# First loads on two queues, w4 in the place of an earlier weight, six output buffers, and a new operation order in an attention and MLP block

## The chip, the cores and the metric

The kernel runs on one core of a Trainium2 chip. The metric is the device time of one execution in microseconds (us); lower is better.

## The reference

One sequence of 2048 rows with 448 features in bf16 goes through two residual blocks. The first is attention over a short sliding window (16 heads of 28 features, 8 keys at distances 0, 2, ... 14 back); the second normalises, mixes neighbouring rows by shifting four groups of features, and ends in an MLP.

```python
S, D, F, H, W, dil = 2048, 448, 1792, 16, 8, 2
# block A
q, k, v = split_heads(layernorm(x) @ wqkv)            # wqkv: 448 x 1344
idx = s - 2*j, j = 0..7, masked where negative
logits[s, j] = (q[s] . k[idx]) * Dh**-0.5
h = x + concat_heads(softmax(logits) @ v[idx]) @ wo   # wo: 448 x 448
# block B
g = gelu(layernorm(h) @ w1)                            # w1: 448 x 448
# the four quarters of g's columns are shifted by +1, -1, +2, -2 rows
x1 = h + shifted(g) @ w2                               # w2: 448 x 448
y = x1 + gelu(layernorm(x1) @ w3) @ w4                 # w3: 448 x 1792, w4: 1792 x 448
out = h + y
```

All eight inputs and the output are bf16 in HBM.

## The kernel before

**Operations and their order.** The kernel is first written down as 891 operations, each one instruction or a short group of instructions on one engine, and only then put in order. `_Sched.add` and `group` record an operation with its dependences; `ORDER` (line 19 on) is one long list of operation numbers, and each engine (PE, the vector engine DVE, ACT, POOL, and SP, which issues the DMAs) executes its own operations in that order, waiting on semaphores for the others. Because every instruction is emitted in one helper, nearly all have the line L994 in the profile; they are told apart by the names of their tiles. `OTHER` (line 51 on) lists operations that are given to a second choice of engine: a copy out of PSUM goes from ACT to DVE (`copy`), the product that ends a softmax from DVE to POOL, one normalisation of four from ACT to DVE. Numbers in `ORDER` and `OTHER` count the operations as they are recorded; w4's two loads are recorded at another place after the change, so that the same operation can have another number there.

**Stages.** The rows are handled in four parts t of 512 rows (four tiles of 128). For each part the operations are recorded in these phases, whose names the text uses with the part's number behind them:

- N1: the first layer norm. DVE's bn_stats and bn_aggr per tile (`ln_stats`), a power on ACT or POOL, the normalisation into `lntm`. In part 0 the work is done tile by tile: tile 0, tile 1, and tiles 2 and 3 together (`FIRST`).
- A1: transposition of `lntm` on PE into `actT`, with copies out of PSUM (`transposed`, `transposed_single`), and the matmuls for q and k with `wqkv_s`, evicted into the arena. V is the same for v, evicted to `vt`; `vw<-vt` are four DMA transfers per part (named vwp, vwa, vwb, vwc) that lay v out by window.
- A2: four products of q with shifted k on DVE (`qk_r`) and their sums over features on PE. S: the softmax on these logits; its last product writes `pb` from the exponentials and the inverse sums, and PE turns it.
- A3: four block-diagonal products on DVE (`bd_r`), PE's matmuls of these with `vw`, copies to `actT`. O: the matmul with `wo_s` and the first residual, added by PE in parts 0 and 1 and by DVE in parts 2 and 3, into `xin`.
- B1: the second layer norm, whose `lntm` is transposed by a DMA (`dma_start_transpose` on SP) into `actT`. M: the matmuls with w1 and gelu, into the arena.

After these come five units u of 2, 4, 4, 4 and 2 tiles:

- B2: the matmul with w2 and the second residual into `xb` in the arena; T: the third layer norm and its transposition by DMA.
- W3: 14 groups of matmuls with w3, each followed by a gelu on ACT into `h3T`.
- B3: the matmul with w4, and DVE's scalar_tensor_tensor into an output buffer `ost`, which SP's DMA stores. There are `NO` = 3 such buffers.

The names T0 or B11 stand for the phase and its part or unit: B11 is phase B1 of part 1, T0 is phase T of unit 0. The order written in `ORDER` interleaves the phases of different parts, so that one part's DVE work stands beside another part's matmuls.

**Buffers.** Tiles come from pools of fixed size (eight PSUM banks, two `lntm`, four `actT`, two `qk_r`, three `bd_r`, sixteen `h3T`, three `ost`); `arrange` hands them out in the order of `ORDER`, and an operation that takes a used buffer waits for the operations that last used it. The weights w3, wqkv with a rearranged copy of part of it (`wr_s`), and w4 lie side by side in one arena in SBUF (`A_W3`, `A_W`, `A_W4`).

**DMAs.** All DMAs are issued by SP, in `ORDER`'s order: x in six pieces (x0 and x1 of one tile, x2, x4 and x6 of two, x8 and x12 of four), the q and k columns of wqkv in two halves (wqka, wqkb), the v columns in two (wv), then wo, w1, w2, w3 in two halves of 896 KB and w4 in two of 784 KB. `load_x` and `load_rows` (lines 428 to 436) record them. `arrange` ties the transposing DMAs to the others on SP:

```python
if op.insts[0][0] == "dma_start_transpose":
    op.deps.update(turned + moved)
    turned, moved = [op], []
elif op.is_dma and not callable(op.chan):
    op.deps.update(turned)
    moved.append(op)
```

A transposing DMA waits until every load and every `vw` transfer that stands ahead of it since the last transposition has landed, and those that stand behind it wait for it. Stores of the output are left out of this. In the order before, the first DMAs are x0, x1, x2, wqka, wqkb, x4, x6 and the two of wv; w3 and w4 stand after the loads of part 0, w4's ahead of T0's transposition.

**Tables.** ACT loads a function table when it goes from exponentials and logarithms to gelu or back; `emit_engine` asks for the first of the two (line 989), the other load is put in by the compiler (line 994).

Of the kernel before, what the change touches and what calls it, by code (L numbers as in the profile page):

```python
# [5 lines left out]
ACT = mybir.ActivationFunctionType  # L6
# [9 lines left out]
NBD, NLN, NACT, NSM, NO = 3, 2, 4, 1, 3  # L16
# [33 lines left out]
"""  # L50
OTHER = """
104 127 196 197 199 402 408 411 519 525 528 582 583
# [229 lines left out]
def bass_sequential_preLN__sliding_local_dilated__mixer_s_mlp__prompt_kernel(  # L282
# [20 lines left out]
    MOVED = {0: (64, 48, 3), 1: (96, 32, 4), 2: (64, 16, 3)}  # L303


    A_W3 = 0
    A_W = A_W3 + 4 * 1792
    A_W4 = A_W + 4 * (1344 + 128)
    A_QG = A_W4 + NF * 448
    QGW = SEQ + 4  # L310
    A_KV = A_QG + 4 * QGW
    KVB = 4 * D * 2
    A_END = A_KV + NST * KVB
    assert 4 * KVW + 1024 <= KVB

    with ExitStack() as es:
# [111 lines left out]
        def load_x(i, n):  # L428
            return dma("x%d" % i, xin[:, i:i + n, :], xv[:, i:i + n, :], 128 * n * D * 2)
# [606 lines left out]
```

## Time and profile before

| | us |
|---|---|
| median of 3 runs | 193.6 |
| lowest and highest run | 193.39, 193.7 |
| span of the profiled execution | 192.0 |
| busy in that span, PE | 181.2 |
| busy, ACT | 133.0 |
| busy, DVE | 129.6 |
| busy, POOL | 29.3 |
| busy, PE's weight loads (beside its matmuls) | 92.6 |

The span runs from the first to the last instruction that the hardware profiler recorded; for the profiled execution this span is its only time, and the runs above are timed without a profile. PE is TensorE, DVE is VectorE, ACT is ScalarE, POOL is GpSimd and SP is SyncE, whose queue (SPq) issues DMAs. In the profile's lines `out<-in` are the program's names of the tiles, `128x512` is partitions by elements, `x4` is the number of instructions, and `<-` names what ended a wait. The granted clock is a share of TensorE's full speed. Inferred waits name what came last.

### The profile page before, as it was taken

How to read it: one execution, taken by the hardware profiler on the slowest of the kernel's cores; microseconds unless marked ns; L12 is line 12 of the kernel's file. 1: busy time of each engine (PE TensorE's matmuls, PEld its weight loads, DVE VectorE, ACT ScalarE, POOL GpSimd, SP SyncE). 2: the span in 40 equal slices, each digit the busy share in tenths (PEclk: the TensorE clock that was granted, in tenths of full speed). 3: DMA queues.
4: the chain of work that ended last, by engine and by line, in shares of the span. 5: the costliest groups of instructions: out<-in, count | busy, mean ns of one | idle time of the engine just before them, and what ended most of it. 6: DMA issues, size and time to landing. Idle time of an engine off the chain costs nothing.

```text
span 192.0 us, 5741 instructions
## 1 busy us (share of the span) xinstructions
PE 181.2 (94%) x2482; PEld 92.6 (48%) x2482; DVE 129.6 (67%) x229; ACT 133.0 (69%) x310; POOL 29.3 (15%) x63
## 2 busy tenths in 40 slices
PE   6999999999999869969999999999999999999994
PEld 2584533453444333337545444455444544555672
DVE  7899999999999999999876970036988022002203
ACT  4489999999999999998595898860158004731340
POOL 3240000000004000201067000022077700000000
DMA  5998792005504163935905014006200542000111
GB/s 146 353 282 175 194 295 44 14 0 133 133 3 90 23 66 72 319 64 125 113 3 106 8 34 103 0 0 126 58 26 1 109 106 73 0 3 0 51 48 48
DMA packets 30273, 17.04 MB, mean 89 GB/s; under 512 B 18936, under 2 KB 29736, under 8 KB 30248
## 3 DMA queue, kind: packets, MB, share of 16 engines
q1 hardware_dynamic: 30248, 16.68, 37.1%
q8 instruction: 19, 0.31, 0.7%
q14 instruction: 6, 0.05, 0.1%
HBM read 8.04 MB, written 1.84 MB: 51 GB/s over the span
## 4 chain that ended last, share of the span: by engine, by line
PE 67%; DMA 13%; ACT 12%; DVE 3%; SPq 2%; issue 1%; POOL 0%; POOLq 0%; ACTq 0%
PE ps L994 67%; DMA actT<-lntm 7%; DMA arena<-in_B_w_dram 3%; ACT lntm L994 3%; ACT arena L994 3%; DMA vw<-vt 2%; ACT vt L994 2%; SPq L994 2%; DVE bd_r L994 2%; ACT h3T L994 1%; ACT actT L994 1%; ACT xin L994 1%; DVE lntm L994 1%; DVE ost L994 1%; ACT ls L994 1%
## 5 line engine op out<-in xcount | busy, mean ns | idle before, releaser
L994 PE MATMUL ps<-actT,arena 64*128 64x256 bf16 (+1 forms) x756 | 68.7, 329 | 2.2 <-DMA actT<-lntm 1.7
L994 ACT ACTIVATE h3T<-ps 128x512 bf16<-128x512 f32 (+1 forms) x70 | 30.3, 525 | 40.1 <-PE ps L994 40.0
L994 PEld LDWEIGHTS ps<-actT,arena 64*128 64x128 bf16 x756 | 35.4, 94 | 31.6 <-DMA actT<-lntm 2.1
L994 PE MATMUL ps<-arena,h3T 64*128 64x448 bf16 (+2 forms) x434 | 44.4, 343 | 0.0
L994 ACT ACTIVATE arena<-ps 128x512 bf16<-128x512 f32 (+10 forms) x86 | 40.1, 515 | 3.3 <-PE ps L994 2.5
L994 DVE SCALAR_TENSOR_TENSOR ost<-ps,mrs,arena 128x448 bf16<-128x448 f32 (+1 forms) x17 | 10.7, 652 | 36.5 <-PE ps L994 36.5
L994 DVE TENSOR_TENSOR qk_r<-arena 128x4096 bf16<-128x4096 bf16 (+1 forms) x16 | 32.0, 2016 | 0.4 <-ACT arena L994 0.2
L994 PEld LDWEIGHTS ps<-arena,h3T 64*128 64x128 bf16 (+1 forms) x434 | 23.0, 94 | 18.7 <-issue 0.2
L994 POOL TENSOR_TENSOR arena<-arena,xin 128x448 f32<-128x448 f32 x16 | 17.2, 1088 | 45.0 <-DVE lntm L994 45.0
L994 DVE TENSOR_TENSOR bd_r<-arena,bmask 80x2048 bf16<-80x2048 bf16 x16 | 19.0, 1216 | 1.6 <-PE ps L994 0.9
L994 ACT ACTIVATE actT<-ps 128x512 bf16<-128x512 f32 (+2 forms) x21 | 14.6, 742 | 2.1 <-PE ps L994 2.1
L994 PE MATMUL ps<-actT,w_s 64*128 64x512 bf16 x112 | 13.3, 377 | 1.7 <-DMA actT<-lntm 1.2
L994 PE MATMUL ps<-wo_s,actT 64*128 64x448 bf16 x128 | 14.3, 350 | 0.1
L994 PE MATMUL ps<-arena,actT 64*128 64x448 bf16 x112 | 12.4, 350 | 0.4 <-ACT vt L994 0.4
L994 PE MATMUL ps<-w_s,arena 64*128 64x448 bf16 x112 | 11.6, 350 | 1.0 <-ACT arena L994 0.9
L994 ACT ACTIVATE lntm<-xin,nm 128x448 bf16<-128x448 bf16 x16 | 10.5, 660 | 2.6 <-DVE nm L994 2.6
L994 DVE SCALAR_TENSOR_TENSOR arena<-xin,rs_y,ps 128x448 f32<-128x448 bf16 x16 | 10.3, 672 | 2.2 <-PE ps L994 2.2
L994 DVE TENSOR_SCALAR lntm<-arena,mv,rs_y 128x512 bf16<-128x512 f32 x14 | 10.2, 773 | 2.1 <-POOL rs_y L994 2.0
L994 POOL TENSOR_TENSOR pb<-ls,mx 128x512 bf16<-128x512 f32 x2 | 3.3, 1641 | 52.8 <-ACT mx L994 52.8
L994 DVE BATCH_NORM_STATS2 st<-xin 128x6 f32<-128x448 bf16 x16 | 9.4, 614 | 0.8 <-DMA xin<-in_A_x_dram 0.7
L994 PEld LDWEIGHTS ps<-actT,w_s 64*128 64x128 bf16 x112 | 5.1, 94 | 8.9 <-PE ps L994 1.7
L994 PEld LDWEIGHTS ps<-wo_s,actT 64*128 64x128 bf16 x128 | 5.6, 94 | 6.7 <-PE ps L994 1.4
(73 smaller groups left out, 161.7 us busy)
## 6 DMA issues: line engine op xcount, KB each, us to landing
arena<-in_B_w_dram SPq DMA_DIRECT2D x2, 896.0 KB, 7.3
out_dram<-ost SPq DMA_DIRECT2D x15, 112.0 KB, 1.9
arena<-in_B_w_dram SPq DMA_DIRECT2D x2, 784.0 KB, 5.7
vw<-vt SPq DMA_DIRECT2D x4, 320.0 KB, 4.3
vw<-vt SPq DMA_DIRECT2D x4, 256.0 KB, 4.2
arena<-in_A_wqkv_dram SPq DMA_DIRECT2D x2, 448.0 KB, 4.6
xin<-in_A_x_dram SPq DMA_DIRECT2D x2, 448.0 KB, 7.5
xin<-in_A_x_dram SPq DMA_DIRECT2D x3, 224.0 KB, 5.6
```

The source lines that it names most:

```text
L994: inst = getattr(eng, meth)(**kw)
```

## The change

The first two loads of x and the two halves of the q and k weights alternate between SP's and ACT's DMA queues: x0 and wqka on SP, x1 and wqkb on ACT; x2 follows wqka on SP, where before it came ahead of it. The first exponential on ACT, which loads a table, and DVE's bn_stats are ordered behind the second half's issue (`odeps`: order only, without a wait; DVE's bn_stats only have to stand behind it in `ORDER`). All loads are ordered one behind the other whatever their queue.

w4 is placed where wqkv and `wr_s` lie (`A_W4 = A_W`), and its two loads are recorded after phase V of part 3, the last that reads those weights; they wait for that. There are six output buffers in place of three.

`ORDER` is a new list throughout, and `OTHER` too. By `OTHER`, eight copies out of PSUM go from ACT to DVE (one of the two for `actT` of tiles 2 and 3 in A10, four in the evictions of q and k, two in A32, one of V3) and four from DVE to ACT (the other of A10's two, one in A32, two in A33). The last products of S0 and S1 go from DVE to POOL, so that all four are there. In B10 one normalisation goes to DVE and another to ACT. ACT has ten table loads where it had twelve. Some steps change places with their neighbours: a bn_stats of tile 4 stands ahead of the normalisations of tiles 2 and 3; B11's normalisations stand behind one block-diagonal product more; T0's normalisations stand ahead of A23's last product of q and k, and six groups of W30's matmuls ahead of PE's sums of that product. SP's order becomes x0, wqka, x2, x4, x6, wv, x8, x12, `vw` of parts 0 and 1, wo, w1, w2, w3's first half, B10's transposition, w3's second half, B11's, T0's, w4's first half, part 3's four `vw` transfers, w4's second half, B12's transposition, T1's, and the rest.

The diff, without the middle of the two order lists:

```diff
--- before.py
+++ after.py
@@ -13,43 +13,43 @@
 TURN = {'A1': 'tttt', 'B1': 'dddd', 'B2': 'ddddd'}
 NORM = {'N0': 'vvvv', 'N1': 'avvv', 'B1': 'avvv', 'B2': 'avvvv'}
 STATS = {'N1': 'vvva', 'B1': 'avaa', 'B2': 'avvvv'}
-NBD, NLN, NACT, NSM, NO = 3, 2, 4, 1, 3
+NBD, NLN, NACT, NSM, NO = 3, 2, 4, 1, 6
 POWER = {'N1': 'aaaa', 'B1': 'aaaa', 'B2': 'apapp'}
 RESIDUAL = 'ttvv'
 ORDER = """
-43 8 7 2 11 0 1 49 44 45 6 9 10 12 5 39 13 40 42 58 59 60 61 63 64 62 70 68 50 51 52 53 54 55 56 57 14 65 66 71 69 67
...
+37 5 0 1 6 7 4 2 38 47 48 49 50 51 52 53 54 55 8 9 10 11 56 57 61 58 59 62 39 60 63 64 40 95 96 97 65 98 100 99 105 13
...
 """
 OTHER = """
-104 127 196 197 199 402 408 411 519 525 528 582 583
+104 125 127 159 195 196 197 251 278 354 363 400 406 412 415 493 519 582 583
 """
 FULL = (4,)
 FILL = (1, 1, 0, 0)
@@ -305,8 +305,8 @@
 
     A_W3 = 0
     A_W = A_W3 + 4 * 1792
-    A_W4 = A_W + 4 * (1344 + 128)
-    A_QG = A_W4 + NF * 448
+    A_W4 = A_W
+    A_QG = A_W4 + max(NF * 448, 4 * (1344 + 128))
     QGW = SEQ + 4
     A_KV = A_QG + 4 * QGW
     KVB = 4 * D * 2
@@ -425,20 +425,21 @@
         xv = x2.rearrange("(i p) d -> p i d", p=128)
         ov = o2.rearrange("(i p) d -> p i d", p=128)
 
-        def load_x(i, n):
-            return dma("x%d" % i, xin[:, i:i + n, :], xv[:, i:i + n, :], 128 * n * D * 2)
-
-        def load_rows(chan, dst, src, lo, n):
+        def load_x(i, n, eng="sp"):
+            return dma("x%d" % i, xin[:, i:i + n, :], xv[:, i:i + n, :], 128 * n * D * 2, eng)
+
+        def load_rows(chan, dst, src, lo, n, engs=("sp", "sp")):
 
             for h in range(2):
-                dma("%s%s" % (chan, "ab"[h]), dst[:, 2 * h:2 * h + 2, :], src[192 * h:192 * h + 256, lo:lo + n].rearrange("(c k) n -> k c n", k=128), 256 * n * 2)
+                dma("%s%s" % (chan, "ab"[h]), dst[:, 2 * h:2 * h + 2, :], src[192 * h:192 * h + 256, lo:lo + n].rearrange("(c k) n -> k c n", k=128), 256 * n * 2, engs[h])
 
         S.tag = "load"
-        for i in range(2):
-            load_x(i, 1)
+        for i, eng in enumerate(("sp", "act")):
+            load_x(i, 1, eng)
+        load_rows("wqk", wqkv_s[:, :, 0:2 * D], A_wqkv, 0, 2 * D, ("sp", "act"))
+        begun = S.ops[-1]
         load_x(2, 2)
-        act(zs[:, 0, 0:1], epsilon[:, 0:1], ACT.Exp)
-        load_rows("wqk", wqkv_s[:, :, 0:2 * D], A_wqkv, 0, 2 * D)
+        act(zs[:, 0, 0:1], epsilon[:, 0:1], ACT.Exp).odeps.add(begun)
         load_x(4, 2)
         load_x(6, 2)
         load_rows("wv", wqkv_s[:, :, 2 * D:3 * D], A_wqkv, 2 * D, D)
@@ -453,13 +454,9 @@
         for k, (lo, c, src, n) in enumerate(((0, 2, 368, 80), (80, 2, 0, 48), (0, 3, 48, 64), (64, 3, 48, 64))):
             dma("w2%d" % k, w2_s[lo:lo + n, c, :], B_w2[src:src + n, :], n * D * 2)
         load_rows("w3", w3_s, B_w3, 0, F)
-        w4_v = B_w4.rearrange("(f k) n -> k f n", k=128)
-        for f in range(0, NF, 7):
-            dma("w4%d" % f, w4_s[:, f:f + 7, :], w4_v[:, f:f + 7, :], 128 * 7 * D * 2)
-        for eng in ("sp", "pool", "act"):
-            loads = [op for op in S.ops if op.tag == "load" and op.eng == eng]
-            for a, b in zip(loads, loads[1:]):
-                b.odeps.add(a)
+        loads = [op for op in S.ops if op.is_dma]
+        for a, b in zip(loads, loads[1:]):
+            b.odeps.add(a)
 
         TOP, BOT = slice(0, 64), slice(64, 128)
 
@@ -495,7 +492,7 @@
 
         def ln_stats(kind, src_ap, i):
             st = _Tile(P_st)
-            dve("bn_stats", out=st(), in_=src_ap)
+            dve("bn_stats", out=st(), in_=src_ap).odeps.add(begun)
             dve("bn_aggr", out=mv[:, kind, i, :], in_=st())
 
         def sums_stats(kind, tiles, src, ln, at=0):
@@ -870,6 +867,11 @@
         UNITS = [range(0, 2), range(2, 6), range(6, 10), range(10, 14), range(14, 16)]
         b2_a = {}
 
+        def load_w4():
+            w4_v = B_w4.rearrange("(f k) n -> k f n", k=128)
+            for f in range(0, NF, 7):
+                dma("w4%d" % f, w4_s[:, f:f + 7, :], w4_v[:, f:f + 7, :], 128 * 7 * D * 2)
+
         def phase_B2(u):
             tiles = UNITS[u]
             summed = STATS["B2"][u] == "a"
@@ -965,6 +967,9 @@
                 for name, phase in phases:
                     S.tag = "%s%d" % (name, t)
                     phase(t)
+                    if S.tag == "V%d" % (NST - 1):
+                        S.tag = "w4"
+                        load_w4()
                     if S.tag == "N10":
                         last = S.ops[-1]
                         S.tag = "late"
```

58 rows, old and new, of the table ORDER are left out of this document.

## The prediction

> **What bounds the kernel now.** I read the page first, then the busy time by window, then the chain of waits, then the timeline at the few places where the chain leaves the matmuls.
>
> ```profile
> span 192.0 us, 5741 instructions
> PE 181.2 (94%) x2482; PEld 92.6 (48%) x2482; DVE 129.6 (67%) x229; ACT 133.0 (69%) x310; POOL 29.3 (15%) x63
> ...
> 0.00:8.19 8.19, 6.23 (x27) 2.74 (x28) 6.29 (x18) 4.41 (x11) 1.67 (x12) 1.00 0.76 228
> 0.00:8.81 8.81, 6.85 (x39) 3.36 (x41) 6.52 (x19) 4.50 (x11) 2.25 (x14) 1.00 0.78 238
> 0.00:58.98 58.98, 56.25 (x921) 27.94 (x922) 55.93 (x85) 52.72 (x139) 5.25 (x37) 1.00 0.55 144
> 0.00:74.18 74.18, 68.47 (x1165) 33.56 (x1165) 70.89 (x109) 67.58 (x171) 7.46 (x38) 1.00 0.54 129
> 0.00:85.71 85.71, 77.98 (x1256) 37.01 (x1257) 81.73 (x130) 78.94 (x197) 8.78 (x40) 1.00 0.55 135
> 0.00:96.07 96.07, 87.85 (x1494) 44.06 (x1494) 90.73 (x145) 86.44 (x218) 10.02 (x42) 1.00 0.56 132
> 15.00:57.00 42.00, 41.30 (x739) 18.58 (x733) 41.69 (x46) 41.73 (x112) 0.00 (x0) 1.00 0.45 110
> 96.00:189.00 93.00, 92.93 (x986) 48.30 (x987) 37.99 (x84) 46.66 (x93) 19.26 (x21) 1.00 0.20 45
> ```
>
> A window's row has start and end, length, the busy time (and instructions) of PE, PE's weight loads, DVE, ACT and POOL, then the granted clock, the DMA engines' share and GB/s. A row from zero gives an engine's work done by then, and time less work is its idle time so far. For PE that is 1.96 us at 8.19, 2.73 at 58.98, 5.71 at 74.18, 7.73 at 85.71 and 8.22 at 96.07. Then it stops: 92.93 of the next 93 us are busy. So the kernel's time is PE's work (181.2), PE's idle time up to 96 us (8.2), and a tail after the last matmul (192.0 - 181.2 - 8.2 = 2.6, the last store). The change alters no matmul and keeps the last stores in their order, so work and tail stay; **only the 8.2 can move**. From 15 to 57 us PE, DVE and ACT are busy 41.30, 41.69 and 41.73 of 42.00: nothing there can swallow a delay. The chain shows where the rest of the 8.2 arises:
>
> ```profile
> 67.50 1.29 DVE lntm L994 x4
> ...
> 68.82 5.27 DMA actT<-lntm
> ...
> 76.09 6.49 DMA arena<-in_B_w_dram
> ...
> 82.60 3.06 DMA actT<-lntm
> ...
> 90.60 5.43 DMA actT<-lntm
> ...
> 96.07 92.72 PE ps L994 x981
> ```
>
> DVE's work (B11's normalisations, to 68.79) sets when B11's transposing DMA starts (68.82); w4's second half, ahead of T0's on SP, sets when that one starts (82.60); B12's starts at 90.60 and PE runs freely from 96.07.
>
> The three runs shown have a median of 193.6; the profiled execution has its span alone, 192.0, so 1.6 us are taken as lying around the span.
>
> **The first loads.** They gain no bandwidth: x0 to x6 and wqk are one stretch of a full DMA system.
>
> ```profile
> 2.00:8.81 6.81, 6.57 (x39) 3.23 (x39) 5.60 (x18) 3.30 (x11) 1.15 (x5) 1.00 0.99 305
> ...
> 0.81 1.34 SPq L994 DMA_DIRECT2D xin<-in_A_x_dram  x3
> ...
> 3.95 0.29 ACT L994 ACTIVATE rs_x<-mv,epsilon 128x1 f32<-128x1 f32 x1 [1.65 <-DVE mv L994]
> ...
> 6.80 0.70 DVE L994 TENSOR_SCALAR lntm<-xin,mv,rs_y 128x448 bf16<-128x448 bf16 x2 [0.32 <-ACT rs_y L994]
> ...
> 7.99 0.42 DVE L994 COPY actT<-ps 128x512 bf16<-128x512 bf16 x1 [0.17 <-PE ps L994]
> 8.19 5.81 PE L994 MATMUL ps<-actT,arena 64*128 64x256 bf16 x98 [0.24 <-issue]
> 8.81 2.34 DVE L994 BATCH_NORM_STATS2 st<-xin 128x6 f32<-128x448 bf16 x4 [0.39 <-DMA xin<-in_A_x_dram]
> ```
>
> The DMA engines are busy 0.99 of the time, so what is issued earlier only lands ahead of something else. The Trainium skill, DMA: Bandwidth & Descriptors, section Issuing engines are not separate DMA queues, says the same of any pair of queues: the transfers interleave on the same 16 engines and only issue time is saved. By that rule x4 lands no earlier than now; by the opposite it would land about 1 us sooner, and the sum below would be 1.1 lower. No run here shows two queues.
>
> x4 lands at about 8.8 now (DVE waits for it until 8.81), and x0, x1, wqk, x2, x4 are the same bytes in the new order, so 8.8 stays. But x2 now follows half of wqk on SP's queue, and the new order puts a bn_stats of tile 4 ahead of the normalisations of tiles 2 and 3. DVE then waits for x4 with two normalisations (0.70) and a copy (0.42) undone: 6.52 - 0.70 - 0.42 = 5.40 of work at 8.85, idle 3.45 instead of 2.29, **1.1 us worse**. PE does 24 matmuls on tiles 0 and 1 (24 x 5.81/98 = 1.4; work 6.23 + 1.4 = 7.65), then waits for the actT copies of tiles 2 and 3: stats 9.4, normalised 10.1, turned and copied 11.3; idle 3.65 instead of 1.96. Bounds: 0 if x2 and x4 land a microsecond earlier, 2 if x2 falls behind all of wqk and x4 behind both. I take 1.1, by x4's row.
>
> ```profile
> L989 ACT ACT_TABLE_LOAD x6 | 7.7, 1283 | 0.9 <-PEq L1021 0.8
> ```
>
> ACT's own two issues cost 2 x 0.45 us (1.34/3 on SP) ahead of its table load (1.28): 0.8 + 0.9 + 1.3 = 3.0, before its first use of the variance at 3.95. Free; at three times the price it would be 0.9 late.
>
> **The order on DVE up to 80 us.** Adding the durations along the new list, DVE has these amounts ahead of each milestone:
>
> ```profile
> L994 DVE CAST actT<-ps 128x512 bf16<-128x512 f32 x4 | 2.7, 683 | 0.0
> L994 DVE TENSOR_TENSOR pb<-ls,mx 128x512 bf16<-128x512 f32 x2 | 1.4, 682 | 0.0
> L994 DVE TENSOR_TENSOR bd_r<-arena,bmask 80x2048 bf16<-80x2048 bf16 x16 | 19.0, 1216 | 1.6 <-PE ps L994 0.9 <-ACT arena L994 0.6
> L994 POOL TENSOR_TENSOR pb<-ls,mx 128x512 bf16<-128x512 f32 x2 | 3.3, 1641 | 52.8 <-ACT mx L994 52.8
> ...
> 57.27 1.05 DVE L994 TENSOR_SCALAR lntm<-xin,nm,rs_y 128x512 bf16<-128x512 bf16 x3
> ...
> 63.60 3.67 PE L994 MATMUL ps<-actT,w_s 64*128 64x512 bf16 x28 [0.77 <-DMA actT<-lntm]
> ...
> actT<-lntm SPq DMA_TRANSPOSE x9, 4.4
> ```
>
> To B10's last normalisation: five more PSUM copies net (0.1 to 0.68 each, 2.1 together), two softmax products given to POOL (-1.2 net of overlap): +0.9. To B11's last: a block-diagonal product (1.14 net) comes ahead as well: +2.1. To A23's last product: +3.9, as another copy (0.6), T0's normalisations (0.9) and two of O2's sums (1.2) come ahead too; PE's work ahead of its use grows by 2.5 (W30's first six groups). To T0's normalisations: -2.9.
>
> The products on POOL take 1.64 on the mean against 0.68. S0's stands between ACT's last exponential and PE's turn with no cover left, and the three engines feed one another from 15 to 57 us without slack, so a delay of one becomes a delay of all. Between 0 and 0.6 us is carried on; I take 0.5. DVE's idle time, 3.05 at 58.98 now, becomes 3.05 + 1.1 + 0.5 = 4.65.
>
> ```profile
> 78.21 1.23 DVE L994 TENSOR_TENSOR qk_r<-arena 128x2048 bf16<-128x2048 bf16 x1
> 79.35 1.00 DVE L994 TENSOR_SCALAR lntm<-arena,nm,rs_y 128x512 bf16<-128x512 f32 x2
> ...
> 80.36 0.40 PE L994 MATMUL ps<-qk_r,zc 128*32 128x512 bf16 x4
> ```
>
> Then, by DVE's present end, its added work and the 1.6 of idle time, with PE's work ahead in brackets:
> B10 is normalised at 58.3 + 0.9 + 1.6 = 60.8 (the row at 57.27 ends at 58.32) and transposed in 4.4; M0 at 65.3, where now it is 63.60. PE's idle time there is 2.73 + 0.77 = 3.5 now, its work 60.1; half a microsecond of that goes behind M0: 65.3 - 59.6 = 5.7.
> B11 at 68.8 + 2.1 + 1.6 = 72.5; 5.27 more, M1 at 77.8 (68.5 + 1.7 of O2 moved ahead = 70.2): idle 7.6, now 5.71.
> T0 at 80.35 - 2.9 + 1.6 = 79.0 and, w4 no longer being ahead of it, transposed in 3.06; W30 at 82.1 (it stands 3.9 of work earlier, 78.0 - 3.9 = 74.1): idle 8.0, now 7.73.
> A23's product at 79.4 + 3.9 + 1.6 = 84.9 (80.36 - 5.7 + 2.5 = 77.1): idle 7.8.
>
> **w4, w1 to w3.** w4's 1.6 MB leave T0's way: the stall at 85.71 is no longer theirs. But the loads of w1, w2 and w3a now stand on SP just ahead of B10's transposition, w3b between it and B11's, and w4 with V3's four vw transfers between T0's and B12's. A transposition waits for every load issued before it.
>
> ```profile
> arena<-in_B_w_dram SPq DMA_DIRECT2D x2, 896.0 KB, 7.3
> arena<-in_B_w_dram SPq DMA_DIRECT2D x2, 784.0 KB, 5.7
> ```
>
> w3b is issued at 65.3 and lands 7.3 later, 72.6, just when B11 is normalised: 0. w4a goes at 82, w4b behind the vw issues at 86; it lands 5.7 to 7 later, 92 to 93. B12: PE ends its B21 group at 79.7 of work, 87.7; DVE has 5.6 from there to B12's last normalisation, 93.3, and 5.43 later, at 98.8, PE has done 90.7: idle 8.1. A33's products, 5 us of DVE work behind, need 8.1 as well. The four vw transfers could put w4b's landing 0 to 2 later; I take 0, since DVE ends as late.
>
> **The rest.**
>
> ```profile
> L994 DVE SCALAR_TENSOR_TENSOR ost<-ps,mrs,arena 128x448 bf16<-128x448 f32 (+1 forms) x17 | 10.7, 652 | 36.5 <-PE ps L994 36.5
> ```
>
> Six output buffers: DVE's wait ahead of ost, 36.5, is all for PE, none for a store, so more of them give 0. Two of the twelve table loads (1.28 each) go, both after 96 us where ACT is busy 46.66 of 93: 0.
>
> **The sum.** Five waits now end at 7.6 (M1), 7.8 (A23), 8.0 (T0), 8.1 (B12) and 8.1 (A33) of idle time. Each is good to half a microsecond; the time goes by the latest, which of five near-equal ones lies about 0.6 above their level of 7.9. With 0.2 for short waits where the new order brings other instructions together (the 8.22 at 96.07 now stands half a microsecond over the 7.73 of T0's wait, by such) that is 8.7 against 8.2: span 192.5, **194.1 us**, slower by 0.26%; alone it ends between 193.3 and 194.9. A difference under 0.2% (0.4 us) can't be told from none here.
>
> **Rivals.** (1) The start costs nothing: x2 and x4 land a microsecond sooner, since wqk is issued at 1.3 instead of 2.2 and 2.7. Then all five waits fall by 1.1: idle 7.6, 193.0 us (192.3 to 193.2), as T0's wait for w4 is gone and nothing has replaced it. Against it: the 0.99. (2) Slower, by one mechanism: w4b and the four vw transfers land after B12 is normalised. It decides from 93.3 us on; each microsecond later is one on the time, as PE's order has nothing else left, 195.3 at 94.5 (194.8 to 196). For it: 2.2 MB go in that stretch, against 6.49 us for w4b alone in the chain. Against it: at the 305 GB/s of the first stretch they need 7.2 us. (3) The gaps close: PE's idle time between 57 and 96 us, 5.5 now, shrinks to 0.5, on the 2.73 + 1.7 brought along: 4.9, 190.3 us. Against it: DVE's four microseconds more ahead of A23's product. (4) The change doesn't bring its loads earlier at all: that is the forecast's own start, as it counts on no bandwidth.
>
> The Trainium skill, SBUF — State Buffer, section Who interferes with whom, has an exclusive lock between GpSimd and a DVE product of two SBUF operands, the later one waiting. The trace agrees: the POOL product that started inside a q·k product took 2.2 us, the one beside bn_stats 1.1.
>
> ```profile
> 58.98 2.28 DVE L994 TENSOR_TENSOR qk_r<-arena 128x4096 bf16<-128x4096 bf16 x1
> ...
> 59.99 2.21 POOL L994 TENSOR_TENSOR pb<-ls,mx 128x512 bf16<-128x512 f32 x1 [47.99 <-ACT mx L994]
> ...
> 86.13 1.07 POOL L994 TENSOR_TENSOR pb<-ls,mx 128x512 bf16<-128x512 f32 x1 [4.84 <-ACT mx L994]
> ```
>
> By that rule S1's product, which stands beside q·k products, takes the 2.2; with 1.1 the carried 0.5 would be 0 and the time 193.6.
>
> **How the numbers follow.** Forecast 0.45 (0.32 slower, 0.13 the same), the free start 0.29 (0.28 faster, 0.01 the same), late w4 0.19 (slower), the closed gaps 0.07 (faster). That makes faster 0.35, the same 0.14, slower 0.51. From 192.3 to 196.0 these are held but for their edges and the last, which is left out.
>
> **What would show it.** Right: DVE's bn_stats of tile 4 near 8.8 with the normalisations of tiles 2 and 3 behind it; a PE gap of about 2 us near 9; PE idle 3.6 by 12 us; M0 near 65, M1 near 77.8, W30 near 82; PE without gaps from about 99; no wait of DVE for a store. Wrong: tiles 2 and 3 normalised before 9, PE's idle time at 57 us below 3.2, or a single wait after 85 us of over 1 us.

## The result, and the profile after

The kernel after the change takes 196.75 us (median of 4 executions, 196.30 to 197.48) against 193.65 before: ratio 1.0149, 95% interval 1.0114 to 1.0184. It is slower by 1.5%. The forecast was 194.1 with a range from 192.3 to 196.0. Executions of a kernel that took over 1.5% longer than its fastest are left out of the ratios, and of the counts further down.

The page of the profiled execution (196.55 us) first, then its busy time by window. The windows are those shown of before; the columns are time, length, busy us (instructions) of PE, PE's weight loads, DVE, ACT and POOL, the granted clock, the DMA share and GB/s.

```profile
span 194.5 us, 5754 instructions
PE 181.8 (93%) x2482; PEld 93.1 (48%) x2482; DVE 128.2 (66%) x231; ACT 130.9 (67%) x304; POOL 33.7 (17%) x65
```

```profile
0.00:8.81 8.81, 6.31 (x35) 2.50 (x35) 6.08 (x17) 4.05 (x10) 1.08 (x10) 1.00 0.83 270
0.00:58.98 58.98, 53.78 (x853) 27.45 (x853) 53.70 (x81) 48.70 (x128) 10.39 (x39) 1.00 0.48 129
0.00:74.18 74.18, 65.59 (x1136) 32.92 (x1138) 67.91 (x105) 62.72 (x159) 11.47 (x40) 1.00 0.46 122
0.00:85.71 85.71, 75.99 (x1248) 37.87 (x1250) 79.33 (x128) 73.69 (x183) 12.70 (x42) 1.00 0.45 116
0.00:96.07 96.07, 86.07 (x1390) 43.67 (x1392) 87.98 (x144) 83.73 (x209) 15.03 (x46) 1.00 0.49 127
96.00:189.00 93.00, 92.83 (x1075) 47.46 (x1071) 38.70 (x85) 47.27 (x96) 18.72 (x19) 1.00 0.24 50
```

Time less PE's work is PE's idle time: 2.50 us at 8.81 (1.96 before), 5.20 at 58.98 (2.73), 8.59 at 74.18 (5.71), 9.72 at 85.71 (7.73) and 10.00 at 96.07 (8.22). So PE is 2.5 us behind by 59 us, stays 1.8 to 2.9 behind, and from 96 us on it is busy without a gap in both kernels. Most of the loss is not where the prediction looked, among the waits from 60 to 96 us, but in one place ahead of them. The windows from 45 to 55 us show it, before first:

```profile
45.00:55.00 10.00, 9.93 (x180) 4.41 (x178) 9.90 (x10) 9.90 (x31) 0.00 (x0) 1.00 0.52 121
```

```profile
45.00:55.00 10.00, 8.08 (x98) 3.66 (x98) 7.76 (x7) 7.59 (x25) 4.03 (x1) 1.00 0.76 177
```

PE, DVE and ACT each lose 2 us, and POOL works 4. The timeline of the kernel after (start, length, engine; in brackets the idle time before and what ended it), DVE, POOL and PE from 44 us:

```profile
44.25 2.29 DVE L999 TENSOR_TENSOR qk_r<-arena 128x4096 bf16<-128x4096 bf16 x1
46.45 0.62 DVE L999 CAST vt<-ps 128x448 bf16<-128x448 f32 x1
46.98 2.29 DVE L999 TENSOR_TENSOR qk_r<-arena 128x4096 bf16<-128x4096 bf16 x1
51.50 1.22 DVE L999 TENSOR_TENSOR bd_r<-arena,bmask 80x2048 bf16<-80x2048 bf16 x1 [2.23 <-ACT arena L999]
...
46.18 4.03 POOL L999 TENSOR_TENSOR pb<-ls,mx 128x512 bf16<-128x512 f32 x1 [9.53 <-ACT mx L999]
...
50.35 0.49 PE L999 MATMUL ps<-ident,pb 64*80 64x64 bf16 x16 [1.86 <-POOL pb L999]
```

S1's last product, which the change gave to POOL, starts at 46.18 while DVE multiplies q by k, and ends at 50.21, 0.94 after DVE's second such product (49.27). PE waits 1.86 us to turn its result, ACT copies that, and DVE waits 2.23 us for the copy. All three lose the same two microseconds in a row.

### The profile page after: what moved, and what is told of

It is laid out like the page before. It is cut to its first block, busy times and chain, and to the rows that moved or that the text cites. A ratio compares the mean times of both kernels' runs of the same rounds, so it can differ in the third digit from the quotient of the medians.

```text
span 194.5 us, 5754 instructions
## 1 busy us (share of the span) xinstructions
PE 181.8 (93%) x2482; PEld 93.1 (48%) x2482; DVE 128.2 (66%) x231; ACT 130.9 (67%) x304; POOL 33.7 (17%) x65
## 3 DMA queue, kind: packets, MB, share of 16 engines
HBM read 8.04 MB, written 1.84 MB: 51 GB/s over the span
## 4 chain that ended last, share of the span: by engine, by line
PE 57%; DVE 28%; ACT 6%; DMA 4%; POOL 2%; issue 1%; SPq 0%; ACTq 0%
PE ps L999 57%; DVE qk_r L999 9%; DVE lntm L999 4%; DVE bd_r L999 4%; DVE st L999 3%; DVE arena L999 3%; DMA xin<-in_A_x_dram 3%; ACT actT L999 2%; POOL pb L999 2%; ACT arena L999 2%; DMA actT<-lntm 2%; DVE mx L999 1%; DVE actT L999 1%; DVE mv L999 1%; DVE ost L999 1%
## 5 line engine op out<-in xcount | busy, mean ns | idle before, releaser
L999 PE MATMUL ps<-actT,arena 64*128 64x512 bf16 (+1 forms) x756 | 70.4, 329 | 1.7 <-DMA actT<-lntm 0.8
L999 PE MATMUL ps<-arena,h3T 64*128 64x448 bf16 (+2 forms) x434 | 45.1, 343 | 0.1
L999 ACT ACTIVATE arena<-ps 128x512 bf16<-128x512 f32 (+10 forms) x83 | 39.2, 505 | 5.1 <-PE ps L999 4.2
L999 ACT ACTIVATE actT<-ps 128x512 bf16<-128x512 f32 (+2 forms) x22 | 15.2, 715 | 6.3 <-PE ps L999 6.1
L999 POOL TENSOR_TENSOR pb<-ls,mx 128x512 bf16<-128x512 f32 x4 | 7.3, 1815 | 56.2 <-ACT mx L999 34.6
L999 PE MATMUL ps<-actT,w_s 64*128 64x512 bf16 x112 | 14.0, 377 | 0.3
L999 DVE TENSOR_SCALAR lntm<-arena,mv,rs_y 128x512 bf16<-128x512 f32 x14 | 7.5, 593 | 3.0 <-ACT rs_y L999 1.9
L999 PE MATMUL ps<-bd_r,vw 80*32 80x64 bf16 x512 | 6.7, 194 | 2.7 <-DVE bd_r L999 1.8
```

Source lines behind the costliest of these rows:

```text
L999: inst = getattr(eng, meth)(**kw)
```

## The experiments

Ratios are to the kernel before, timed beside each kernel.

**S1's product on DVE.** One number less in `OTHER`:

```diff
-104 125 127 159 195 196 197 251 278 354 363 400 ...
+104 125 127 159 195 196 197 251 354 363 400 ...
```

> The kernel after, with S1's last softmax product on DVE again (0.68 us there) in place of POOL, where it took 4.03 us and PE waited 1.86 us for it. Theory (POOL is held up by DVE's two products of q and k that run meanwhile, and PE's wait is a loss that nothing later gives back): PE waits for pb at 50 us no longer, DVE works 0.7 longer, the time falls by 1.2 to 1.9 us to 194.9 to 195.6. Rival (DVE sets the pace from 15 to 75 us anyway, so the 0.68 comes on top of its work and the wait would have been passed on to the next stage in any case): less than 0.5 us, 196.3 or more.

Measured 195.62 us, ratio 1.0076 (1.0040 to 1.0113): half of the loss is gone, at the slow edge of the forecast. DVE's timeline shows why it is only half:

```profile
46.23 0.69 DVE L999 TENSOR_TENSOR pb<-ls,mx 128x512 bf16<-128x512 f32 x1 [1.80 <-ACT mx L999]
46.83 2.28 DVE L999 TENSOR_TENSOR qk_r<-arena 128x4096 bf16<-128x4096 bf16 x1
```

On POOL nobody minded when the product had to wait for ACT's inverse sums. On DVE, at the same place in the list, it holds up the q·k product behind it by 1.80 us.

**The same, one place further back.** The product (278) goes behind the q·k product (388):

```diff
-... 275 276 ... 278 ... 388 493 386 ...
+... 275 276 ... 388 278 493 386 ...
```

> As after_s1_dve, with S1's product moved one product of q and k back on DVE, so that DVE multiplies (2.29 us) while ACT still works on the inverse sums, where in after_s1_dve it waited 1.80 us for them. Theory (the wait that is left in after_s1_dve at 45 to 55 us, PE idle 1.42 there, is DVE's wait for ACT, made by the place of the product in the list): PE's idle time from 45 to 55 us falls to 0.5 or less, 194.3 to 194.9. Rival (DVE's own work there is the limit): PE's idle time there stays above 1 us, 195.4 to 195.9.

Measured 193.95, ratio 0.9993 (0.9971 to 1.0014): the whole loss is gone, and more was in it than the theory expected. DVE's timeline and the window:

```profile
44.59 2.27 DVE L999 TENSOR_TENSOR qk_r<-arena 128x4096 bf16<-128x4096 bf16 x1
46.79 0.68 DVE L999 TENSOR_TENSOR pb<-ls,mx 128x512 bf16<-128x512 f32 x1
47.39 0.61 DVE L999 CAST vt<-ps 128x448 bf16<-128x448 f32 x1
```

```profile
45.00:55.00 10.00, 9.94 (x146) 4.51 (x142) 10.00 (x9) 9.64 (x29) 0.00 (x0) 1.00 0.72 163
```

DVE is busy 10.00 of 10.00 us and PE 9.94. By the ratios, one product of 0.68 us on the wrong engine costs 1.0149/0.9993, 1.6% or 3.0 us. Between executions whose mean granted clock is 1.00 it is 2.5 us (medians 196.43 of two and 193.94 of twelve), which is nearer to the two microseconds of the timelines; half of the executions of the kernel after have a clock of 0.99, none of those with the product here (see the last section).

**The same product on POOL in the kernel before.**

```diff
-104 127 196 197 199 402 ...
+104 127 161 196 197 199 280 402 ...
```

> The kernel before, with the last softmax products of S0 and S1 on POOL, at the places that they have in its order. Theory (beside DVE's products of q and k the one on POOL lasts as long as they do, 2 to 4 us, and PE waits for it): one of the two takes over 2 us on POOL, PE's idle time from 15 to 57 us grows from 0.7 to 1.5 or more, 194.5 to 196.5. Rival (DVE is relieved of 1.4 us in a stretch in which it has no slack): 192.3 to 193.6.

Measured 194.24, ratio 1.0014 (0.9982 to 1.0046): neither of the two forecasts. The timeline of POOL and DVE, and the window:

```profile
32.21 1.11 POOL L994 TENSOR_TENSOR pb<-ls,mx 128x512 bf16<-128x512 f32 x1 [20.90 <-ACT mx L994]
44.72 3.65 POOL L994 TENSOR_TENSOR pb<-ls,mx 128x512 bf16<-128x512 f32 x1 [10.94 <-ACT mx L994]
...
32.31 3.16 DVE L994 TENSOR_TENSOR qk_r<-arena 128x4096 bf16<-128x4096 bf16 x1
...
42.95 4.47 DVE L994 TENSOR_TENSOR qk_r<-arena 128x4096 bf16<-128x4096 bf16 x2
```

```profile
45.00:55.00 10.00, 9.93 (x180) 4.40 (x176) 9.26 (x8) 9.83 (x31) 3.41 (x2) 1.00 0.52 121
```

S1's product takes 3.65 us, again ending 0.95 after a q·k product (47.42). S0's came first, at 32.21, and here it is DVE's product, begun 0.1 later, that takes 3.16 us in place of 2.28. But from 45 to 55 us PE is busy 9.93 of 10, as it is without, and from 15 to 57 us its idle time grows only from 0.70 to 0.99: the old order has other work for PE in that stretch. So it takes both, a product that lasts as long as DVE's beside it and an order that has PE turn it at once.

**x2 ahead of the weights.** The loads of x2 and of the q and k weights change places in the kernel after:

```diff
+        load_x(2, 2)
         load_rows("wqk", wqkv_s[:, :, 0:2 * D], A_wqkv, 0, 2 * D, ("sp", "act"))
         begun = S.ops[-1]
-        load_x(2, 2)
```

> The kernel after, with x2 issued ahead of the first half of the q and k weights on SP (x0, x2, wqka on SP; x1, wqkb on ACT), all else the same. Theory (the start's loss is x2's place: it landed at 6.75 in place of 4.54, and the normalisations of tiles 2 and 3 follow it): PE idle by 15 us falls from 2.96 to 2.0 to 2.3, and the time by 0.6 to 0.9, 195.5 to 196.1. Rival 1 (wqkb on ACT's queue now lands earlier or later than the first matmuls need it, and they wait for the weights instead): PE idle by 15 us stays at 2.7 or more, 196.3 to 197. Rival 2 (what is won at the start is waited away at S1's product on POOL): idle by 15 us falls, the time stays within 0.3 of 196.6.

Measured 196.01, ratio 1.0087 (1.0058 to 1.0116). By the ratios that is 0.6% or 1.2 us of the loss; by the medians 0.7. The time came as forecast, PE's idle time did not: at 15 us it is 15 - 11.77 = 3.2, no less than the 2.96 after. What comes sooner is the rest: by 15 us DVE has done 12.19 us of work (11.99 after) and ACT 7.91 (7.62), and by 100 us PE's idle time is 9.36 (10.06 after).

**Both in one kernel, on two queues and on one.**

> after_s1_dve_behind and after_x2_first in one kernel: S1's product on DVE, behind a product of q and k, and x2 issued ahead of the first half of the q and k weights, on two queues. Theory (two separate losses: the wait for POOL at 50 us, and the late x2, that together are what the change lost): the gains add up, 193.95 less 0.7, 193.0 to 193.5, and as the order then has no loss of its own it is faster than before. Rival (DVE's work ahead of B11 to B12 sets the end in either case, the start is hidden): 193.7 to 194.2.

> As mix_two_queues, but with the four first loads on SP alone, in the order of the kernel before (x0, x1, x2, then both halves of the weights). Theory (all first loads share one stream of full bandwidth, so the order counts and not the queue; the second queue costs 0.1 us outside the span): within 0.3 us of mix_two_queues, 192.7 to 193.6. Rival (two queues save issue time that the start feels): slower than mix_two_queues by 0.4 us or more.

Two queues: 193.13, ratio 0.9939 (0.9913 to 0.9965), **faster than the kernel before**, and the best of all. The two losses add up: the kernel after has 1.0149, the product's way back gives 0.9993/1.0149 = 0.9846 and x2's 1.0087/1.0149 = 0.9939, and 1.0149 x 0.9846 x 0.9939 is 0.9932, against 0.9939 measured. One queue: 194.02, ratio 0.9984 (0.9955 to 1.0013), so here the rival was right: with this order the second queue is worth 0.9 us. PE's timeline on one queue, and DVE's on one and then on two, say by what:

```profile
8.00 1.05 PE L999 MATMUL ps<-actT,arena 64*128 64x256 bf16 x16 [1.04 <-DMA arena<-in_A_wqkv_dram]
...
8.61 0.63 DVE L999 BATCH_NORM_STATS2 st<-xin 128x6 f32<-128x448 bf16 x1 [1.68 <-DMA xin<-in_A_x_dram]
9.15 0.69 DVE L999 TENSOR_SCALAR lntm<-xin,mv,rs_y 128x448 bf16<-128x448 bf16 x2
```

```profile
7.76 0.63 DVE L999 BATCH_NORM_STATS2 st<-xin 128x6 f32<-128x448 bf16 x1 [0.20 <-DMA xin<-in_A_x_dram]
8.30 0.69 DVE L999 TENSOR_SCALAR lntm<-xin,mv,rs_y 128x448 bf16<-128x448 bf16 x2
```

The weights' second half lands at 7.91 there and PE's first real matmuls wait 1.04 us for it; on two queues it lands at 5.52, but PE comes to them only 0.21 us sooner (7.79), as it then waits for ACT's copy. More is lost behind: DVE's bn_stats of tile 4 waits 1.68 us for x4 (0.20 on two queues), and the normalisations of tiles 2 and 3 that stand behind it end 0.85 us later. By 15 us PE has been idle for 3.33 us there, 2.22 on two queues. That is the wait that the prediction had put into the kernel after.

**Two queues alone, and one queue alone.** First the kernel before with x1 and the weights' second half on ACT's queue, ahead of its table load; then the kernel after with all its loads on SP.

```diff
-        for i in range(2):
-            load_x(i, 1)
+        for i, eng in enumerate(("sp", "act")):
+            load_x(i, 1, eng)
...
-        load_rows("wqk", wqkv_s[:, :, 0:2 * D], A_wqkv, 0, 2 * D)
+        load_rows("wqk", wqkv_s[:, :, 0:2 * D], A_wqkv, 0, 2 * D, ("sp", "act"))
```

> The kernel before, with x1 and the second half of the q and k weights issued by ACT ahead of its table load, x2 still ahead of the first half on SP, all else as before. Theory (a fixed cost outside the span for the second queue, 0.45 us, and x2 shares the bandwidth with the weights and lands some 0.5 us later): time less span 2.0, PE idle by 12 us 2.0 to 2.5 (1.96 before), 194.1 to 194.6. Rival 1 (the start's loss is all due to x2's place behind the first half of the weights and the bn_stats of tile 4 put ahead): PE idle by 12 us 1.96 or less and 193.2 to 193.8. Rival 2 (two queues bring the loads in sooner): under 193.2.

> The kernel after, with x1 and the second half of the q and k weights issued by SP again; the order of the loads stays. Theory (the use of a second DMA queue adds a fixed cost outside the recorded span: 196.55 less a span of 194.5 is 2.05 us, where before it was 193.6 less 192.0, 1.6): the time less the span goes back to 1.6, the span moves by no more than 0.3, so 196.3. Rival 1 (the 0.45 is a matter of which execution was profiled): the time less the span stays at 2.0. Rival 2 (the second queue is what lets x4 land by 8.1 instead of 8.8): the span grows by 0.5 to 1, PE's idle time by 12 us from 2.96 to 3.5 or more.

The first: 194.54, ratio 1.0030 (1.0001 to 1.0058). x4 lands at 7.38 in place of 8.79, and the kernel is no faster: in the old order the normalisations of tiles 2 and 3 stand ahead of tile 4's bn_stats, which waited only 0.39 us for x4 anyway. The second: 196.73, ratio 1.0114 (1.0069 to 1.0158), not to be told from the kernel after. The time outside the span is 1.67 to 1.80 us in the executions of before, 1.78 to 1.84 with two queues in its order, 1.88 to 2.05 after, and 1.75 to 1.83 in all but one execution of after on one queue. By the medians (1.73 and 1.80, 1.82 and 1.98) a second queue goes with 0.1 to 0.2 us more there, not 0.45.

**w4's loads.** In the kernel before they go behind T0's transposition, in the best kernel ahead of it (in the shared place, whose old contents were last read at 60.3 us), and in a third kernel the first half goes one step earlier than before. Only their places in `ORDER` change:

```diff
 before_w4_late:    turn B11, vw, vw, turn T0, w4a, vw, w4b, vw, turn B12
 mix_w4_ahead:      turn B11, w4a, w4b, turn T0, vw x4, turn B12
 before_w4a_early:  turn B10, w4a, turn B11, vw, w4b, vw, turn T0, vw x2, turn B12
```

> The kernel before, with w4's two loads behind T0's transposition on SP, as the change has them, one ahead of and one between part 3's last two vw transfers; w4 keeps its own place in SBUF. Theory (T0's transposition starts when its rows are normalised, 80.4 in place of 82.6; then B12's, which waits for w4's second half and the vw transfers, is the latest wait): W30 starts 1.5 to 2.2 us sooner, B12's transposition starts between 89 and 91 us, 192.6 to 193.9. Rival (1.6 MB of w4 and the vw transfers land after 91 us and B12's transposition waits for them): 194.3 to 195.5.

> mix_two_queues with w4's two loads ahead of T0's transposition on SP, directly behind B11's, where the kernel before has them; w4's place in SBUF stays the shared one (the last matmul on the q, k and v weights ends at 60.3 us, so w4 can land from then on). Theory (in the new order w4's place behind T0 is what lets T0's rows be turned as soon as they are normalised, and B12's transposition, at 92.5 bound by DVE's normalisations at 92.4, loses nothing by it): T0's transposition starts at 82 to 83.5 in place of 77.4, PE waits 2 to 5 us more for W30's first groups, 194.5 to 198. Rival (the order has other work for PE while T0 waits, as in the kernel before): within 0.5 us of mix_two_queues, 192.7 to 193.6.

> The kernel before, with w4's first half one step earlier on SP (between B10's and B11's transpositions, where the DMA engines are idle) and the second half in its place, so that both have landed before T0's rows are normalised. Theory (in before_w4_late it was the room behind T0's transposition that was overfilled, and T0's wait itself is worth something): T0's transposition starts at 80.2 to 80.8 in place of 82.6, the two vw transfers behind it land by 88.5, B12's starts at 88 to 89.8, 192.0 to 193.3. Rival (B12's transposition is bound by DVE's normalisations at 89.8 whatever T0 does): 193.2 to 193.9.

Late in the old order: 200.20, ratio 1.0284 (1.0233 to 1.0335). Ahead in the new order: 200.52, ratio 1.0319 (1.0273 to 1.0364), 7 us slower than with w4 behind T0. Both are slower than theory and rival had it. One step early in the old order: 193.63, ratio 0.9952 (0.9925 to 0.9980), which alone makes the kernel before faster, by as much as the rival said. w4 late in the old order, its chain of waits and PE's wait in the timeline, and then w4 ahead in the new order, the timeline:

```profile
85.14 8.35 DMA vw<-vt
93.54 6.00 DMA actT<-lntm
```

```profile
99.58 1.01 PE L994 MATMUL ps<-actT,w_s 64*128 64x512 bf16 x4 [4.20 <-DMA actT<-lntm]
```

```profile
75.37 0.98 SPq L999 DMA_DIRECT2D arena<-in_B_w_dram  x2
82.23 1.23 SPq L999 DMA_TRANSPOSE actT<-lntm  x1
...
85.48 2.93 PE L999 MATMUL ps<-actT,arena 64*128 64x256 bf16 x25 [5.49 <-DMA actT<-lntm]
```

One step early, T0's transposition starts at 81.27 in place of 82.60 and B12's at 90.50, as before; by 100 us PE has been idle for 7.2 us in place of 8.2. In the old order the load that is spared T0 is paid by B12: its rows are normalised at 89.55, its transposition waits to 93.54, and PE has nothing but M2 left. In the new order PE comes to W30 at 80 and needs T0 by then, whereas it has W30 and B30 to do while B12 is turned. Neither kernel can do with the other's place. Not all of the 7 us is waiting: by 100 us PE has been idle for 4.7 us more than in mix_two_queues (11.28 and 6.62), and behind the wait the granted clock is at half for a while (last section).

Nor do the other parts of the change stand alone. The kernel after with three output buffers in place of six (after_no3), expected within 0.3 us of the kernel after, gave no time: in this order an output tile of B31 is asked for while all three are held. With w4 in a place of its own, SBUF has room for three. What more buffers are worth by themselves is therefore not shown.

## Why the prediction was wrong, point by point

**The step that failed: what S0's and S1's products cost on POOL.** The prediction took 0.5 us for both, bounded at 0.6. S0's costs nothing to be seen (1.08 us, from 35.57 on, beside copies); S1's costs 3.0 by the ratios, 2.5 at a clock of 1.00. The prediction sets the mean of two rows, 1.64, against DVE's 0.68 and gives no working for the 0.6; the longest row seen, 2.21, had one q·k product beside it. The profile of before had the mechanism, though: 2.21 at 59.99 is DVE's product, to 61.26, and 0.94 more. What was left out was to read in the new list what stands beside S1's product on DVE: a q·k product, a copy of 0.62, and another q·k product. By "ends 0.94 after the last of them" it would have come to 4 us, on a path where PE, ACT and DVE hand each other work.

The rule that the prediction cited, the Trainium skill, SBUF — State Buffer, section Who interferes with whom, says that a DVE instruction with two SBUF inputs and a GpSimd one that reads SBUF lock each other out and the later waits. The traces agree both ways round: POOL's product takes 1.08 us without a q·k product beside it (the 1.07 at 86.13 in the kernel before stood beside scalar_tensor_tensors for the larger part, not bn_stats), ends 0.93 to 0.95 us after the last one where it began inside (at 50.21, 48.37 and, before, 62.20; the same in all 16 such places of the 13 profiled kernels), and lengthens DVE's where it began first (3.16). The rule was weighed as a matter of 1.1 or 2.2 us for one lock; two locks in a row gave 4.03.

**The start.** Direction right, reason wrong, size near, the last by luck. The prediction put 1.1 us on DVE's bn_stats of tile 4, waiting for x4 at 8.85; x2 ahead of the weights gives back 0.7 to 1.2. DVE's timeline after:

```profile
3.65 0.63 DVE L999 BATCH_NORM_STATS2 st<-xin 128x6 f32<-128x448 bf16 x1 [1.18 <-DMA xin<-in_A_x_dram]
...
6.78 1.15 DVE L999 BATCH_NORM_STATS2 st<-xin 128x6 f32<-128x448 bf16 x2 [0.32 <-DMA xin<-in_A_x_dram]
7.84 0.30 DVE L999 BATCH_NORM_AGGREGATE mv<-st 128x2 f32<-128x6 f32 x2
8.06 0.59 DVE L999 BATCH_NORM_STATS2 st<-xin 128x6 f32<-128x448 bf16 x1
8.75 0.70 DVE L999 TENSOR_SCALAR lntm<-xin,mv,rs_y 128x448 bf16<-128x448 bf16 x2
```

Tile 4's bn_stats at 8.06 waits for nothing. What waits is tile 2's, to 6.78, and x0's, to 3.65 (3.08 before). The wait for x4 that the prediction priced comes with one queue, 1.68 us in mix_one_queue; with two, x4 doesn't stay at 8.8. So "they gain no bandwidth" was wrong. A DMA share of 0.99 was read as a full system; from 4 to 6 us it is 0.96 with 306 GB/s before, 1.05 with 390 after, and 1.04 with 380 in the kernel after on one queue:

```profile
4.00:6.00 2.00, 2.00 (x10) 0.91 (x7) 1.97 (x6) 0.94 (x4) 0.00 (x0) 1.00 0.96 306
```

```profile
4.00:6.00 2.00, 1.82 (x6) 0.43 (x5) 1.93 (x7) 0.99 (x4) 0.00 (x0) 1.00 1.05 390
```

```profile
4.00:6.00 2.00, 2.00 (x14) 0.93 (x12) 1.65 (x6) 1.12 (x5) 0.00 (x0) 1.00 1.04 380
```

x4 is issued at 2.30 in place of 3.21 and lands at 7.43 in place of 8.79. The Trainium skill, DMA: Bandwidth & Descriptors, section Issuing engines are not separate DMA queues, grants a second engine only the saved time of issuing. The trace agrees: against the same order of loads on one queue, where x4 is issued at 3.22 and lands at 8.34, the issue is 0.92 us sooner and the landing 0.91. The conclusion drawn from it, "no earlier", was the prediction's own. The other 0.45 us, from 8.79 to 8.34, come with the weights standing ahead of x2, on one queue already; by what stays open.

**The order on DVE.** Forecast and measured starts of the transpositions: B10's 60.8 and 61.94, B11's 72.5 and 74.18, T0's 79.0 and 80.79. With S1's product put right (193.95) the rows are normalised at 60.4, 71.5 and 78.2, 1.4 to 2.6 us sooner than after. So the sums of DVE's work held to a microsecond, and what was missing in them is that product. W30 then waited as forecast, 0.82 us for T0's transposition, with PE idle 9.7 by then in place of 8.0. M1 did not wait: its rows landed at 78.45 and PE came to it at 78.74, with 8.7 us of idle time in place of 7.6; its last long waits (1.16 and 0.63 us) were for A32's products on DVE.

**w4.** The second rival, w4's second half landing behind B12's normalisation, stayed away by a hair: it landed at 95.59 (forecast 92 to 93), the rows were normalised at 95.75 (93.3), and the transposition started at 95.81. Some 0.9 us more would not have mattered either: the transposition landed 4.4 us later, at 100.2, and PE, idle 0.06 us from 95 to 100, came to M2 at 101.08. So "PE's order has nothing else left" was wrong for the new order. It was right for the old order, at four microseconds. T0's relief was judged right in kind and too low: the prediction gave it no term of its own, and it is worth 7 us in the order that uses it.

**PE's work** was said to stay. It is 181.8 us against 181.2. Among the kernels profiled at a clock of 1.00 it is 181.1 to 181.4 in the three with the old order and 181.4 to 182.3 in the six with the new one. The same matmuls take longer as a group with the same mean (groups by form, before and after):

```profile
L994 PE MATMUL ps<-arena,h3T 64*128 64x448 bf16 x392 | 38.9, 349 | 0.0
```

```profile
L999 PE MATMUL ps<-arena,h3T 64*128 64x448 bf16 x392 | 39.6, 349 | 0.1
```

Matmuls overlap each other (392 of 349 ns each fill 39 us), and the new order goes from one phase's matmuls to another's 124 times where the old went 104 times. That each such change costs PE some 0.03 us is an estimate from these counts (0.6 us over 20), and a rough one: kernels of the new order differ by 0.9 us among themselves. No run changed it alone.

**The other rivals.** The first had x4 right (it landed more than a microsecond sooner) and x2 wrong. The third, closed gaps, did not come: in mix_two_queues PE is still idle for 4 us between 57 and 98 us.

**The rest** held: no wait of DVE for a store, the table loads free, ACT's two issues free (its first Ln at 4.53 waited for DVE), PE without gaps from 99 us, and the tail of 2.6 us. Against the profiled execution's forecast of 194.1, the 2.45 us too little are 1.4 of PE's idle time (10.06 at 100 us against 8.7), 0.6 of PE's work and 0.45 outside the span (2.05 against 1.6). The 1.6 was a median of runs less the span of one; where an execution of before has both, it is 1.67 to 1.80.

**What the change is worth** without its two losses is in mix_two_queues: 0.6% faster, of which 0.4% are left between executions at a mean clock of 1.00 (193.13 and 193.86). PE's idle time at 100 us is then 6.62:

```profile
0.00:100.00 100.00, 93.38 (x1572) 47.62 (x1574) 95.38 (x157) 86.66 (x215) 13.43 (x46) 1.00 0.50 127
```

against 8.22 before. Of these 1.6 us, 0.6 are there by 74 us and another 0.9 come at T0's wait (6.27 in place of 7.73 once W30 has started).

## What to carry to other kernels

An operation that goes to another engine is priced by what stands beside it there, not by the mean of its like: look up in the new order which instructions of the other engine overlap it, and whether the two hold each other up, as POOL's and DVE's products did here. If its consumers stand right behind it, one such operation can cost three to four times its own length, as here 0.68 us cost 2.5. An order, the places of its loads and its buffers are one design: w4's place is worth 7 us in one order and costs 6 in the other, so a part of such a change is tried with the order that goes with it.

## What the runs showed of the hardware

A product on POOL that reads SBUF made no progress to be seen while DVE multiplied two operands from SBUF, nor in the copy of 0.62 us from PSUM between two such products: 4.03 us where it takes 1.08 alone.

After a stretch in which PE did little, the granted clock fell to half for some microseconds. In the kernel after on one queue, PE does 0.16 us of work from 8 to 10 us, and then:

```profile
8.00:10.00 2.00, 0.16 (x4) 0.00 (x0) 1.91 (x7) 0.50 (x2) 0.00 (x0) 1.00 1.09 374
10.00:12.00 2.00, 1.79 (x24) 1.31 (x26) 2.00 (x6) 0.60 (x1) 1.49 (x9) 0.93 0.87 276
12.00:15.00 3.00, 3.00 (x32) 2.57 (x29) 1.78 (x8) 1.14 (x7) 2.59 (x20) 0.50 0.03 8
```

With w4 ahead in the new order PE does nothing from 80.0 to 85.5 us, and the clock is 0.50 from 82 to 88. It doesn't take one long gap: with w4's first half one step early PE does 0.72 us of work from 68 to 70, with no single wait above 0.68 us, and the clock is 0.50 from 71 to 73.

Whether this happens varies between executions of one kernel. In the kernel after, two executions kept a mean clock of 1.00 (196.30 and 196.55) and two had 0.99 (196.95 and 197.48). Of the kernels with the new order and w4 behind T0, the three with S1's product on POOL had 0.99 in 9 of 20 executions, the four with it on DVE in 1 of 42. So the gap at that product seems to cost clock as well as waiting. Where in the execution the clock falls is not shown: the only one of these ten with a profile, of after on one queue, is the one above, at 12 us and long before that product.

From 4 to 6 us, with x2 ahead of the weights, one queue moved 284 to 316 GB/s and two moved 369 to 397; with the weights ahead of x2, one moved 380 and two 388 to 393. A second queue went with 0.1 to 0.2 us more outside the recorded span.
